# Seven-product units in the first matmul of the last two chunks of a fused attention and squared-ReLU MLP kernel, with a new order of the second matmul's products

## Chip, cores and metric

One Trainium2 chip, one core. The metric is the device time of one execution in microseconds (us). The kernel before took 306.88 us (median of three executions, 306.31 to 307.04).

## What must be computed

The reference, cut to what matters here:

```python
def reference(q, k, v, w_in, w_out):      # q, k, v: 8 batches x 8 heads x 576 x 64
    attn = _attn_ref(q, k, v)             # four heads with a sliding window, four with a dilated one
    x = attn.transpose(0, 2, 1, 3).reshape(4608, 512)
    h = x @ w_in                          # 512 -> 2048    ("mm1")
    r = np.maximum(h, 0.0)
    g = r * r
    return (g @ w_out).astype(np.float32) # 2048 -> 512    ("mm2")
```

## The kernel before

The 4608 tokens are worked in nine chunks of 512, numbered 0 to 8. Attention produces the activations batch by batch. The matmuls of a chunk are generators, and small steps of them are put between the steps of the attention of the next batch. So chunks 1 to 6 run beside attention; chunks 7 and 8 come after it and run alone.

mm1 makes `g` in 16 "p tiles": four matmuls of 512 columns into one bank of PSUM, a relu on ScalarE (ACT), a square on VectorE (DVE):

```python
def mm1_gen(c, g, sm=None):
    for ffc in range(NFF):                                   # 16 tiles
        ph = pmool.tile([P, TOKC], FP32, ..., tag="pm")      # pmool rotates four banks
        for n, dmk in enumerate((2, 3, 0, 1)):
            nc.tensor.matmul(ph, wi[:, dmk, ffc * P : ffc * P + P], xs[:, dmk, :], ...)
        relu_squared(c, ffc, g, ph, rts)
        # ... sums of g for mm2 between the tiles ...
```

mm2 is already a Strassen scheme of seven products. The first product of `a` is read out, and then a second one is added to it in the same bank; so it is with `b`. I write the order of the products as **a d b a b c e**:

```python
a = bank("poa")                                        # bank(): a tile of pmool, tag "pm"
yield from product(a, gv[:, :, 0, 0:HT], B11, True)    # first product into a
nc.scalar.copy(s1, a)                                  # readout by ACT
d_ = bank("pod");  yield from product(d_, gv[:, :, 1, HT:TOKC], T[:, 3], True)
b_ = bank("pob");  yield from product(b_, sm[:, 1], T[:, 1], True)
nc.vector.tensor_add(u2, b_, s1)                       # readout by DVE
yield from product(a, gv[:, :, 1, 0:HT], B21, False)   # second product into a
nc.scalar.copy(otu[:, :, left], a)
yield from product(b_, sm[:, 2], T[:, 2], False)       # second product into b
nc.vector.tensor_add(u3, b_, s1)
nc.vector.tensor_add(otl[:, :, left], d_, u3)
c_ = bank("poc");  yield from product(c_, sm[:, 0], T[:, 0], True)
nc.vector.tensor_add(u2, c_, u2)
nc.vector.tensor_add(otl[:, :, right], c_, u3)
e_ = bank("poe");  yield from product(e_, sm[:, 3], B22, True)
nc.vector.tensor_add(otu[:, :, right], e_, u2)
```

Two PSUM pools matter. `pmool` has four buffers of one bank, shared by mm1, mm2 and some tiles of attention (the transposes `px` and `py` among them). `papool` has two buffers of two banks each, used by attention alone.

The softmax here doesn't subtract the row's maximum and nothing guards it: scores larger than these inputs give would overflow.

## Time and profile before

| | before |
|---|---|
| time, median | 306.88 us |
| span in the trace | 305.5 us |
| TensorE (PE) busy | 296.3 us, 97% |
| a chunk beside attention (chunks 2 to 5, mean) | 30.88 us |
| chunk 7, chunk 8 | 26.04, 26.06 us |

The span is the time from the first to the last instruction on the core; the chain of waits follows what ended last backwards through it. A chunk is measured from the first mm1 matmul of its own in that chain to the first of the next chunk.

These lines are from the timeline of the kernel before, in chunk 5 (start, length, engine, line, operation, result and sources, count, and the idle time before it):

```profile
207.26 0.62 ACT L467 COPY s<-poa 128x512 f32<-128x512 f32 x1
...
209.67 1.04 PE L438 MATMUL poa<-wo,g 128*128 128x256 f16 x8
209.69 0.69 DVE L475 TENSOR_TENSOR u<-pob,s 128x512 f32<-128x512 f32 x1
...
211.93 1.04 PE L438 MATMUL pob<-T,sm 128*128 128x256 f16 x8
...
214.14 0.69 DVE L484 TENSOR_TENSOR u<-pob,s 128x512 f32<-128x512 f32 x1
...
216.45 1.04 PE L438 MATMUL poe<-wo,sm 128*128 128x256 f16 x8
```

The readout of `a` ends at 207.88, and `a`'s second product begins at 209.67: 1.8 us to spare. The readout of `b` ends at 210.38, its second product begins at 211.93: 1.55 us to spare. The readout of `b`'s second product ends at 214.83, and `e` begins at 216.45: 1.6 us, with `c` in between. A product takes 1.75 us where mm2 runs alone and about 2.25 us here, where steps of attention stand between its halves. So each slack is less than one product, and taking away the product that stands in between uses it up.

### The profile page before, as it was taken

Reading aid. Unit: us, or ns where it says so; the run is one execution under the profiler, and the core shown is the slowest. Engines: PE = TensorE matmul, PEld = TensorE weight load, DVE = VectorE, ACT = ScalarE, POOL = GpSimd, SP = SyncE. Lnnn points to the kernel's source line nnn. Section 1 sums busy time; section 2 is a strip of 40 time slices with the busy share of each in tenths; the row PEclk is TensorE's granted clock in tenths of the full one; section 3 lists DMA queues with packets and bytes.
Section 4 is the critical chain, followed back from the end, with each engine's and each line's share of the span. In section 5 each row is a group of like instructions: output and inputs, shape, how many; then the busy total and the mean of one; then the engine's idle time right before and its main releaser. Section 6 shows DMA issues by size and latency. Waiting matters only on the chain.

```text
span 305.5 us, 7013 instructions
## 1 busy us (share of the span) xinstructions
PE 296.3 (97%) x2898; PEld 192.8 (63%) x2898; DVE 208.8 (68%) x410; ACT 185.0 (61%) x308; POOL 48.5 (16%) x97
## 2 busy tenths in 40 slices
PE   8899998999999999999999999999999999999994
PEld 3675444444696469646964697459745974684584
DVE  4653475849966797679766977697769775843744
ACT  6466777478834893489348943894389437405610
POOL 7454013006004100320032003200100010000000
PEclk9999999999999999999999999999999999999999
DMA  8999989899899998689939983989310012003004
GB/s 175 226 213 230 233 174 203 160 232 269 210 191 219 310 170 185 217 182 198 228 111 197 216 184 123 213 184 209 117 72 0 2 61 78 2 0 137 2 0 138
DMA packets 85615, 47.89 MB, mean 157 GB/s; under 512 B 68112, under 2 KB 82896, under 8 KB 85200
## 3 DMA queue, kind: packets, MB, share of 16 engines
q1 hardware_dynamic: 76688, 27.24, 40.8%
q0 software_dynamic: 8352, 19.80, 28.9%
q8 instruction: 22, 0.36, 0.5%
q10 hardware_dynamic: 544, 0.43, 0.5%
q14 instruction: 9, 0.07, 0.1%
HBM read 39.85 MB, written 16.52 MB: 184 GB/s over the span
## 4 chain that ended last, share of the span: by engine, by line
PE 90%; ACT 3%; DMA 3%; POOL 2%; issue 1%; DVE 1%; ACTq 0%; POOLq 0%
PE ph L388 42%; PE pob L438 9%; PE poa L438 9%; PE poe L438 5%; PE poc L438 5%; PE pod L438 4%; PE po L409 4%; DMA early<-in_q_dram 3%; PE paw L776 3%; PE pav L759 2%; PE pz L675 2%; PE ps L656 1%; PE py L809 1%; PE px L791 1%; POOL early L119 1%; ACT AT L628 1%
## 5 line engine op out<-in xcount | busy, mean ns | idle before, releaser
L388 PE MATMUL ph<-xT,wi 128*128 128x512 f16 x576 | 129.8, 379 | 0.0
L354 ACT ACTIVATE rt<-ph 128x512 f16<-128x512 f32 x144 | 84.9, 601 | 36.4 <-PE ph L388 36.1
L388 PEld LDWEIGHTS <-wi 128*128 128x128 f16 x576 | 54.4, 98 | 62.4
L358 DVE TENSOR_TENSOR g<-rt 128x1024 f16<-128x1024 f16 x63 | 43.5, 691 | 47.2 <-ACT rt L354 47.0
L438 PEld LDWEIGHTS <-sm 128*128 128x128 f16 x512 | 46.9, 98 | 4.8
L438 PEld LDWEIGHTS <-g 128*128 128x128 f16 x384 | 35.9, 98 | 6.9 <-DVE g L356 1.3
L438 PE MATMUL pob<-T,sm 128*128 128x256 f16 x256 | 32.5, 272 | 0.0
L438 PE MATMUL poa<-wo,g 128*128 128x256 f16 x256 | 32.4, 273 | 0.0
L458 POOL DMA_DIRECT2D out_dram<-otl x6 | 4.6, 763 | 152.6 <-DVE otl L493 152.6
L815 ACT COPY xT<-py 128x576 f16<-128x576 f16 x16 | 10.2, 640 | 27.3 <-PE py L809 27.3
L740 DVE TENSOR_TENSOR x_d<-paw,rcp_d 72x512 f16<-72x512 f32 x32 | 22.0, 687 | 1.1
L797 ACT COPY xT<-px 128x576 f16<-128x576 f16 x16 | 10.3, 642 | 13.6 <-PE px L791 13.6
L409 PE MATMUL po<-wo,g 128*128 128x512 f16 x64 | 17.8, 379 | 0.0
L735 DVE RECIPROCAL rcp_d<-paw 72x8 f32<-72x8 f32 x32 | 6.4, 199 | 16.2 <-PE paw L776 16.2
L628 ACT ACTIVATE AT<-pz 128x576 f16<-128x576 f32 x28 | 16.6, 652 | 1.0 <-PE pz L675 0.6
L628 ACT ACTIVATE AT<-ps 128x576 f16<-128x576 f32 x28 | 16.6, 649 | 0.5
L740 DVE TENSOR_TENSOR x_p<-pav,rcp_p 96x512 f16<-96x512 f32 (+1 forms) x24 | 16.2, 676 | 0.8
L438 PE MATMUL poe<-wo,sm 128*128 128x256 f16 x128 | 16.3, 273 | 0.0
L438 PE MATMUL pod<-T,g 128*128 128x256 f16 x128 | 16.3, 272 | 0.0
L438 PE MATMUL poc<-T,sm 128*128 128x256 f16 x128 | 16.2, 272 | 0.0
L478 ACT COPY otu<-poa 128x512 f32<-128x512 f32 x8 | 4.7, 586 | 17.5 <-PE poa L438 17.5
L629 DVE TENSOR_TENSOR AT<-AT,maskd 128x576 f16<-128x576 f16 x28 | 12.2, 455 | 3.5 <-ACT AT L628 2.5
(120 smaller groups left out, 354.5 us busy)
## 6 DMA issues: line engine op xcount, KB each, us to landing
sv<-in_v_dram SPq DMA_DIRECT2D x40, 128.0 KB, 3.1
sd<-in_v_dram SPq DMA_DIRECT2D x8, 512.0 KB, 6.2
dk<-in_k_dram POOLq DMA_DIRECT2D x12, 288.0 KB, 7.0
dk<-in_q_dram POOLq DMA_DIRECT2D x12, 288.0 KB, 7.5
out_dram<-otl POOLq DMA_DIRECT2D x6, 512.0 KB, 3.3
out_dram<-otu POOLq DMA_DIRECT2D x6, 512.0 KB, 4.2
sd<-in_v_dram SPq DMA_DIRECT2D x8, 288.0 KB
wi<-in_moe_w_in_dram POOLq DMA_DIRECT2D x4, 512.0 KB, 10.3
```

What stands on the lines that cost most here:

```text
L354: nc.scalar.activation(rt[:, o, :], ph[:], ACTF.Relu)
L358: nc.vector.tensor_mul(g[:, ffc - 1 : ffc + 1, :], rt, rt)
L388: nc.tensor.matmul(ph, wi[:, dmk, ffc * P : ffc * P + P], xs[:, dmk, :], start=(n == 0), stop=(n == NDM - 1),)
L409: nc.tensor.matmul(po, g[:, ffc, t * P : (t + 1) * P], wo[:, ffc, :], start=(ffc == 0), stop=(ffc == NFF - 1),)
L438: nc.tensor.matmul(acc, lhs[:, k, t * P : (t + 1) * P], rhs[:, k, :], start=(first and k == 0), stop=(k == NK - 1), skip_group_check=True,)
L628: nc.scalar.activation(AT[:, u, 0:UW], ps[:, :, 0 : UW // 2], ACTF.Exp, scale=scale)
L629: nc.vector.tensor_mul(AT[:, u, 0:UW], AT[:, u, 0:UW], mask)
L735: nc.vector.reciprocal(rcp[0:w, 0:n], pv[:, :, :, D])
L740: nc.vector.tensor_tensor(out=x[0:w, 0:n], in0=pv[:, :, :, 0:D], in1=rcp[0:w, 0:n].unsqueeze(3).to_broadcast([w, n, HH, D]), op=ALU.mult,)
L776: nc.tensor.matmul(pav[:, e, h * (D + 2) : h * (D + 2) + D + 1], AT[:, u, off : off + P], vd[:, t, 2 * a + e, h, 0 : D + 1], start=True, s ...
L797: nc.scalar.copy(xT[:, 0:2, t0 : t0 + 288], px[:, 0:UW].rearrange("x (c t) -> x c t", c=2),)
L815: nc.scalar.copy(xT[:, 2:4, t0 : t0 + 288].rearrange("x c (i r) -> x c i r", r=DIL), py[:, 0:UW].rearrange("x (c r i) -> x c i r", c=2, r= ...
```

## The change

In mm1 of chunk 7, three groups of four tiles of `g`, and in chunk 8 two, are done as "units": seven products of four 256-column matmuls in place of 16 matmuls of 512 columns. Units need sums of quarters of `w_in` (four for each unit, done late in attention), sums of quarters of x, and more readouts. mm2 gets the order **a d a b c b e** in chunks 1 to 7, so that the sums of `g` are wanted later. The diff, cut to its core:

```diff
+    units = {NTOKC - 2: 3, NTOKC - 1: 2}
+    def w_in_sums(u): ...          # four DVE sums: s1..s4, 128x512 fp16 each
+    def x_sums(c): ...             # four DVE sums: t1..t4
+    def unit_gen(c, u, g):
+        both = papool.tile([P, 2, 2, HT], FP32, name=f"pu{c}_{u}", tag="pa")
+        a, d = both[:, 0], both[:, 1]
+        product(a, w(0, 0), x_quarter(c, 0, 0), True)
+        nc.scalar.copy(m1, a)
+        e = pmool.tile([P, 2, HT], FP32, name=f"pe{c}_{u}", tag="pm")
+        product(e, w(0, 1), x_quarter(c, 1, 0), True)
+        nc.vector.tensor_add(g1[:, :, first], e, m1)
+        product(a, s2, t2, False)
+        nc.scalar.copy(m6, a)
+        product(d, s1, t1, True)
+        finish(g1[:, :, first])                      # relu on ACT, square on DVE
+        product(a, s3, t3, False)
+        nc.scalar.copy(m7, a)
+        nc.vector.tensor_add(g2[:, :, second], d, m7)
+        product(a, w(1, 1), t4, False)
+        nc.scalar.activation(g2[:, :, first], a, ACTF.Relu)
+        product(d, s4, x_quarter(c, 1, 1), False)
+        nc.vector.tensor_add(g1[:, :, second], d, m6)
+        ...
+    orders = {2: "p01010p10p10p1psspspsp", 3: "01010p102120p12p2ssp2ss", ...}
...  (mm2)
-        b_ = bank("pob")                             # b's first product
-        yield from product(b_, sm[:, 1], T[:, 1], True)
-        ...
         yield from product(a, gv[:, :, 1, 0:HT], B21, False)
         nc.scalar.copy(otu[:, :, left], a)
+        if not last:
+            b_ = bank("pob"); ...                    # b's first product, now behind a's second
+            c_ = bank("poc"); ...                    # c, now ahead of b's second
         yield from product(b_, sm[:, 2], T[:, 2], False)
-        c_ = bank("poc"); ...
...  (attention of the last batch)
+        def fill():
+            pump(2)
+            if b == B - 1:
+                for _ in range(2):
+                    next(late_sums, None)            # two sums of w_in behind each step
```

In `orders` a digit is a step of that unit, `p` a p tile, `s` a sum of `g`.

More of the change, by code (lines that the diff above doesn't have):

```diff
@@ L60 @@
     tp = ctx.enter_context(tc.tile_pool(name="tp", bufs=1))
+    kp = ctx.enter_context(tc.tile_pool(name="kp", bufs=1))
     osb = ctx.enter_context(tc.tile_pool(name="osb", bufs=4))
@@ L73 @@
     wo = wpool.tile([P, NFF, DM], FP16, name="wo")
-    QKTp = [const.tile([P, 2, PADP + S], FP16, name=f"QKTp{hp}") for hp in range(2)]
+    QKTp = [kp.tile([P, 2, PADP + S], FP16, name=f"QKTp{hp}", tag=f"k{hp}") for hp in range(2)]
     QKTd = const.tile([P, 2, 2, KPAD + S], FP16, name="QKTd")
-    QKTx = const.tile([P, 2, PADP + HH * S], FP16, name="QKTx")
+    QKTx = kp.tile([P, 2, PADP + HH * S], FP16, name="QKTx", tag="kx")
     AT = const.tile([P, 8, 640], FP16, name="AT")
@@ L406, in mm1_gen, with w_in_sums, quarter @@
             yield
+    units = {NTOKC - 2: 3, NTOKC - 1: 2}
+    HU = 2 * P
+    ws0 = const.tile([P, 4, 2, HU], FP16, name="ws0")
+    ws: list = [ws0]
+    def w_in_sums(u):
+        def quarter(i, j):
+            f0 = 4 * P * u + HU * i
+            return wi[:, 2 * j : 2 * j + 2, f0 : f0 + HU]
+        s1, s2, s3, s4 = (ws[u][:, i] for i in range(4))
+        nc.vector.tensor_add(s1, quarter(1, 0), quarter(1, 1))
+        yield
+        nc.vector.tensor_sub(s2, s1, quarter(0, 0))
+        yield
+        nc.vector.tensor_sub(s3, quarter(0, 0), quarter(1, 0))
+        yield
+        nc.vector.tensor_sub(s4, quarter(0, 1), s2)
+        yield
@@ new lines, in w_in_sums_late, with x_quarter, x_sums @@
+    def w_in_sums_late():
+        wx = kp.tile([P, 2, 4, 2, HU], FP16, name="wsx", tag="kx")
+        ws.extend((wx[:, 0], wx[:, 1]))
+        for u in (0, 1, 2):
+            yield from w_in_sums(u)
+    xsums = {}
+    def x_quarter(c, j, i):
+        t0 = c * TOKC + HT * i
+        return xT[:, 2 * j : 2 * j + 2, t0 : t0 + HT]
+    def x_sums(c):
+        t = [kp.tile([P, 2, 2, HT], FP16, name=f"xs{c}_{n}", tag=f"k{n}") for n in range(2)]
+        t1, t2, t3, t4 = t[0][:, 0], t[0][:, 1], t[1][:, 0], t[1][:, 1]
+        xsums[c] = t1, t2, t3, t4
+        nc.vector.tensor_sub(t1, x_quarter(c, 0, 1), x_quarter(c, 0, 0))
+        nc.vector.tensor_sub(t2, x_quarter(c, 1, 1), t1)
+        nc.vector.tensor_sub(t3, x_quarter(c, 1, 1), x_quarter(c, 0, 1))
+        nc.vector.tensor_sub(t4, x_quarter(c, 1, 0), t2)
@@ new lines, in unit_gen, with w, product, part @@
+    def unit_gen(c, u, g):
+        t1, t2, t3, t4 = xsums[c]
+        s1, s2, s3, s4 = (ws[u][:, i] for i in range(4))
+        f0 = 4 * u
+        g1, g2 = g[:, f0 : f0 + 2, :], g[:, f0 + 2 : f0 + 4, :]
+        first, second = slice(0, HT), slice(HT, TOKC)
+        def w(i, j):
+            c0 = P * f0 + HU * i
+            return wi[:, 2 * j : 2 * j + 2, c0 : c0 + HU]
+        def product(acc, lhs, rhs, start):
+            for n in range(2):
+                for k in range(2):
+                    nc.tensor.matmul(
+                        acc[:, n, :],
+                        lhs[:, k, n * P : (n + 1) * P],
+                        rhs[:, k, :],
+                        start=(start and n == 0 and k == 0),
+                        stop=(k == 1),
+                        skip_group_check=True,
+                    )
+        def part(name):
+            return osb.tile([P, 2, HT], FP32, name=f"{name}{c}_{u}", tag="u")
+        both = papool.tile([P, 2, 2, HT], FP32, name=f"pu{c}_{u}", tag="pa")
+        a, d = both[:, 0], both[:, 1]
+        def finish(x):
+            nc.scalar.activation(x, x, ACTF.Relu)
+            nc.vector.tensor_mul(x, x, x)
+        product(a, w(0, 0), x_quarter(c, 0, 0), True)
+        m1 = part("m1")
+        nc.scalar.copy(m1, a)
+        yield
+        e = pmool.tile([P, 2, HT], FP32, name=f"pe{c}_{u}", tag="pm")
+        product(e, w(0, 1), x_quarter(c, 1, 0), True)
+        nc.vector.tensor_add(g1[:, :, first], e, m1)
+        yield "stage"
+        product(a, s2, t2, False)
+        m6 = part("m6")
+        nc.scalar.copy(m6, a)
+        yield
+        product(d, s1, t1, True)
+        finish(g1[:, :, first])
+        yield "stage"
+        product(a, s3, t3, False)
+        m7 = part("m7")
+        nc.scalar.copy(m7, a)
+        nc.vector.tensor_add(g2[:, :, second], d, m7)
+        yield "stage"
+        product(a, w(1, 1), t4, False)
+        nc.scalar.activation(g2[:, :, first], a, ACTF.Relu)
+        yield
+        product(d, s4, x_quarter(c, 1, 1), False)
+        nc.vector.tensor_mul(g2[:, :, first], g2[:, :, first], g2[:, :, first])
+        nc.vector.tensor_add(g1[:, :, second], d, m6)
+        yield "stage"
+        finish(g2[:, :, second])
+        finish(g1[:, :, second])
@@ new lines, with mm1_units_gen @@
+    orders = {
+        1: "0p0p0p0p0" + "p" + "sp" * 4 + "ppp",
+        2: "p01010p10p10p1psspspsp",
+        3: "01010p102120p12p2ssp2ss",
+    }
+    def mm1_units_gen(c, g, sm, nu):
+        if c not in xsums:
+            x_sums(c)
+        xs = xT[:, :, c * TOKC : (c + 1) * TOKC]
+        rts = {}
+        stages = [unit_gen(c, u, g) for u in range(nu)]
+        sums = hidden_sums(g, sm, 0, NK // 2)
+        ffc = 4 * nu
+        for step in orders[nu]:
+            if step == "p":
+                ph = pmool.tile([P, TOKC], FP32, name=f"ph{c}_{ffc}", tag="pm")
+                for n in range(NDM):
+                    nc.tensor.matmul(
+                        ph,
+                        wi[:, n, ffc * P : ffc * P + P],
+                        xs[:, n, :],
+                        start=(n == 0),
+                        stop=(n == NDM - 1),
+                    )
+                    if n == 1:
+                        yield
+                relu_squared(c, ffc, g, ph, rts)
+                ffc += 1
+                yield
+            elif step == "s":
+                next(sums)
+            else:
+                for what in stages[int(step)]:
+                    yield
+                    if what:
+                        break
+        assert ffc == NFF
+        for _ in sums:
+            pass
+        for _ in hidden_sums(g, sm, NK // 2, NK):
+            pass
+        yield
@@ L471, in mm2_strassen_gen @@
         yield
-        b_ = bank("pob")
-        yield from product(b_, sm[:, 1], T[:, 1], True)
-        u2 = part("u2")
-        nc.vector.tensor_add(u2, b_, s1)
-        yield
+        if last:
+            b_ = bank("pob")
+            yield from product(b_, sm[:, 1], T[:, 1], True)
+            u2 = part("u2")
+            nc.vector.tensor_add(u2, b_, s1)
+            yield
         yield from product(a, gv[:, :, 1, 0:HT], B21, False)
@@ L481, in mm2_strassen_gen @@
         yield
+        if not last:
+            b_ = bank("pob")
+            yield from product(b_, sm[:, 1], T[:, 1], True)
+            u2 = part("u2")
+            nc.vector.tensor_add(u2, b_, s1)
+            yield
+            c_ = bank("poc")
+            yield from product(c_, sm[:, 0], T[:, 0], True)
+            nc.vector.tensor_add(u2, c_, u2)
+            yield
         yield from product(b_, sm[:, 2], T[:, 2], False)
@@ L487, in mm2_strassen_gen @@
             put(1, otl, nc.sync, left)
-        yield
-        c_ = bank("poc")
-        yield from product(c_, sm[:, 0], T[:, 0], True)
-        nc.vector.tensor_add(u2, c_, u2)
+            yield
+            c_ = bank("poc")
+            yield from product(c_, sm[:, 0], T[:, 0], True)
+            nc.vector.tensor_add(u2, c_, u2)
         nc.vector.tensor_add(otl[:, :, right], c_, u3)
         put(1, otl, out_eng, right if last else slice(0, DM))
+        if c + 1 == NTOKC - 1:
+            x_sums(c + 1)
         yield
@@ L531, in moe_gen @@
         sm = gp.tile([P, 4, NK, HT], FP16, name=f"sm{c}", tag="sm")
-        yield from mm1_gen(c, g, sm)
+        if c in units:
+            yield from mm1_units_gen(c, g, sm, units[c])
+        else:
+            yield from mm1_gen(c, g, sm)
         yield from mm2_strassen_gen(c, g, sm)
@@ L1011 @@
         pump(3)
-        attn_values(b, lambda: pump(2))
+        if b == B - 1:
+            late_sums = w_in_sums_late()
+        def fill():
+            pump(2)
+            if b == B - 1:
+                for _ in range(2):
+                    next(late_sums, None)
+        attn_values(b, fill)
         pump(1000)
```

## The prediction

> **What bounds the kernel now.** I read the page first: the busy row, the slices and the chain that ended last.
>
> ```profile
> PE 296.3 (97%) x2898; PEld 192.8 (63%) x2898; DVE 208.8 (68%) x410; ACT 185.0 (61%) x308; POOL 48.5 (16%) x97
> ...
> PE   8899998999999999999999999999999999999994
> ...
> PE 90%; ACT 3%; DMA 3%; POOL 2%; issue 1%; DVE 1%; ACTq 0%; POOLq 0%
> ```
>
> TensorE (PE) is busy 97% and is 90% of the chain, so only matmul time removed, or a new wait put in front of a matmul, moves the end. Next, the chain in order of time, at its last pieces: chunk 7 (first five lines) and the end of chunk 8 (last two).
>
> ```profile
> 249.50 13.81 PE ph L388 x64
> 263.32 1.75 PE poa L438 x16
> 265.06 1.75 PE pod L438 x16
> 266.81 1.75 PE pob L438 x16
> 268.56 1.75 PE poa L438 x16
> ...
> 298.09 1.75 PE poc L438 x16
> 299.84 1.76 PE poe L438 x16
> ```
>
> The columns are start, length, group and count. So mm1 of a chunk is 64 matmuls in 13.81 us, 0.216 us each at 512 columns. A Strassen product of mm2 is 16 matmuls of 256 columns in 1.75 us, 0.109 us each. A chunk is 13.81 + 7 x 1.75 = 26.06 us, and nothing waits in it. Third, the busy time of each engine by stage: attention with chunk 6's mm2, chunk 7's mm1, chunk 7's mm2.
>
> ```profile
> 234.17:249.34 15.17, 15.17 (x198) 13.66 (x196) 12.72 (x26) 7.63 (x11) 0.00 (x0) 1.00 0.01 2
> 249.34:263.15 13.81, 13.81 (x66) 6.27 (x64) 7.98 (x13) 8.96 (x15) 1.45 (x2) 1.00 0.20 76
> 263.15:275.38 12.23, 12.23 (x114) 10.96 (x112) 6.77 (x11) 1.77 (x3) 0.00 (x0) 1.00 0.00 1
> ```
>
> After the length the columns are PE, PE's weight loads, VectorE (DVE), ScalarE (ACT). PE is full in all; DVE has only 2.4 us left in the first. Last, the durations of single operations, from the groups of the last 56 us by shape, and two pieces of the timeline:
>
> ```profile
> L354 ACT ACTIVATE rt<-ph 128x512 f16<-128x512 f32 x32 | 19.1, 597 | 14.6 <-PE ph L388 14.6
> ...
> L343 DVE TENSOR_TENSOR sm<-g 128x1024 f16<-128x1024 f16 x4 | 2.8, 692 | 0.1
> ...
> L356 DVE TENSOR_TENSOR g<-rt 128x512 f16<-128x512 f16 x4 | 1.7, 426 | 1.2 <-ACT rt L354 1.2
> ...
> L475 DVE TENSOR_TENSOR u<-pob,s 128x512 f32<-128x512 f32 x2 | 1.4, 691 | 3.2 <-PE pob L438 3.2
> ```
>
> The two pieces of the timeline (start, length, engine, operation, idle before it):
>
> ```profile
> 227.79 1.09 ACT L354 ACTIVATE rt<-ph 128x512 f16<-128x512 f32 x2
> ...
> 250.40 0.60 ACT L354 ACTIVATE rt<-ph 128x512 f16<-128x512 f32 x1 [1.10 <-PE ph L388]
> ```
>
> An ACT evacuation of 512 columns lasts 0.60 us; two queued ones take 1.09, so the next starts after 0.50. Four matmuls begun at 249.34 are issued by 250.20 and ACT starts at 250.40: 0.20 us from PE to ACT. DVE: 0.43 for 512 fp16 values, 0.69 for 1024 fp16 or for 512 from PSUM; in queued rows of the timeline the next starts 0.08 before the end. I use 0.03 to 0.05 us from ACT or DVE to the next engine.
>
> [...]
>
> **The change part by part.**
>
> *Removed.* A group is 16 matmuls of 512 (16 x 0.2158 = 3.45 us); a unit is 28 of 256 (28 x 0.1094 = 3.06). It saves 0.39; five units save **1.95 us**, all on the bounding engine.
>
> *Added on ACT and DVE.* A unit has 7 ACT ops (three copies m1, m6, m7, four relus) instead of 4, and 7 DVE ops (three adds from PSUM, four squares) instead of 2. Chunk 7 then needs in mm1 about 25 x 0.50 = 12.5 us of ACT, and on DVE 4 x 0.40 (sums of x) + 9 x 0.62 + 12 x 0.38 + 1.4 + two sums of g at 0.65 = 14.4 us, against 12.6 us of PE work. Both engines that had been 58 to 65% busy become as full as PE.
>
> *Added: a wait inside each unit.* I compared the order of instructions and the waits of both builds. Each unit's a and d are halves of one PSUM tile, and the first matmul of d = S1 T1 waits for the ACT copy m6 of a, though it writes d; likewise d += S4 x22 (the last quarter of x) waits for the ACT relu of a. Each such pair has a product of a immediately ahead, so PE must sit through 0.20 (PE to ACT) + 0.60 (ACT) + 0.05 = **0.85 us**, twice a unit. Ten times: 8.5 us. Interleaving the other unit does not help: it is not between these two products.
>
> *Moved: twelve sums of w_in* go into the last attention values, two after each step, at 0.35 to 0.46 each: 4.5 us into 2.4 of room. I walked DVE's queue with the durations above from the last sum of g (start 237.44). x_p2, on which the transposes px need, is done at 240.63 instead of 239.8: PE 0.2 late. The fourth step's sums and the fifth's stand together, so x_d of step d0_1 is done at 247.5 instead of 245.1. The paw after it needs the buffer that this frees: PE 1.4 later. Then py_1 waits for the bank that u3 frees (250.4): 0.7 more. Sum **+2.3 us**.
>
> *Chunk 7, walked the same way* (PE starts at 0; a pair of products takes 0.875, a p tile 0.863). Pairs for units 0 and 1 run to 1.75. M6 of unit 0 ends 2.19, its copy 2.99, d runs 3.04 to 3.48 (0.85 lost). Unit 1: a to 3.92, d from 4.77 (0.85). Then M7 and p to 6.51, M7 of unit 1 to 6.95. ACT runs late now: m7 of unit 0 done 6.45, the add on it 7.17, so unit 0's last a starts at 7.22 (0.27 lost), d at 8.51 (0.85). Unit 2 needs unit 0's tile, which the add d + m6 frees at 9.84: 0.94 lost. Unit 1's last d: 0.85; unit 2's first d: 0.85, PE at 14.22. Two p and M7 to 16.38; m7 of unit 2 stands behind four relus and a p on ACT, done 17.38, its add 18.1: 1.77 lost. Last d: 0.85; last p ends 20.74. In mm2 the second product waits for the last square of unit 2 (23.15): 0.27. Lost: 6 x 0.85 + 0.27 + 0.94 + 1.77 + 0.27 = 8.35; saved 3 x 0.39 = 1.17; **+7.2 us**.
>
> *Chunk 8*, two units among eight p tiles: 4 x 0.85, about 0.05 more at one of them, 0.27 before unit 0's last a, and 1.0 in the first product of mm2, which comes to tiles 12 and 14 before ACT (about 3 us behind) and DVE have squared them. Lost 4.75, saved 0.78: **+4.0 us**. The later order of mm2's products in chunks 1 to 7 moves no PE work and should cost nothing there.
>
> *Sum:* 306.9 + 2.3 + 7.2 + 4.0 = 320.4; I say **320.0 us**.
>
> **The rivals.** *First, the saving comes through.* PE is 97% busy and the units are interleaved to hide ACT; then 306.9 - 1.95 = 304.9. Against it stand the waits in the build: even with every other queue infinitely fast, ten times 0.85 less 1.95 gives 313.4. *Second, ACT and DVE throughput bind, and the waits inside the units are mostly covered by that.* Chunk 7's DVE work of 14.4 us plus about 1 us of start would end mm1 about 2 us later than now, chunk 8 about even, the attention stage +2.3: some 311. For it: both engines are nearly full. Against: PE's order is fixed, so a wait of PE also starves ACT of work; waits add, not overlap. *Third, my walk compounds too much:* if ACT's relus from SBUF are faster than evacuations, or the DVE sums cost nothing at the end of attention, I lose the 1.77, 0.94 and 2.3 but keep the ten waits: about 315.
>
> **Range and chances.** The floor from the ten waits is 313.4, already 2.1% over; all terms give 320.4. Chains longer than walked ([...]ACT working off its lag slower) add up to 4. So 315 to 324. Faster needs the waits not to exist: 0.01. Within 2% (up to 313.0) needs a mistake about half of them: 0.06. Slower: 0.93.
>
> **What would show it.** The profile after should have PE's idle time at the matmuls of d released by ACT (copies m6, relus of g), ten times, near 0.85 us each; a larger wait before unit 2's first and last a, released by DVE; ACT and DVE over 85% busy in chunk 7's mm1; matmul time down by 2 us; chunk 7 about 33 us long, chunk 8 about 30; PE gaps at paw and py in the last attention. If PE shows no gap there, the step of the shared tile is wrong; if mm1 of chunk 7 takes 16 us instead of 20.7, the queue walk is too pessimistic; if the attention stage keeps its 15.2 us, DVE's room was misjudged.

Of the range, the "up to 4" for longer chains remains as the author's estimate. The 0.03 to 0.05 us from ACT or DVE to the next engine is an estimate, too; the trace of the kernel before shows 0.03 from a relu on ACT that ends at 251.87 to the DVE operation at 251.90.

## The result

The changed kernel took **327.13 us** (median of four executions, 326.49 to 332.15), the kernel before 306.81 in the same rounds. The ratio is 1.0658 (95% interval 1.0625 to 1.069). Ratios here are the mean time of one kernel's fast runs over that of the other's of the same rounds, so not quite the ratio of the medians. One execution of the four, at 332.15 with a clock of 0.988, is left out of the ratio; the median of the three fast ones is 326.55, and differences from the changed kernel are taken from it below. The direction was predicted; the time lies 7 us above the prediction and outside its range of 315 to 324.

The page of the kernel after (busy row, PE and clock slices, shares of the chain):

```profile
PE 299.8 (92%) x2958; PEld 199.4 (61%) x2958; DVE 227.3 (70%) x455; ACT 191.8 (59%) x323; POOL 48.5 (15%) x97
...
PE   7999998999899999999999999999999765997995
PEclk9999999999999999999999999999999999799999
...
PE 59%; ACT 13%; DVE 12%; DMA 10%; issue 4%; SPq 1%; POOL 0%; ACTq 0%; POOLq 0%; DVEq 0%
```

PE falls from 97% to 92%, and from 90% of the chain to 59%: ACT and DVE now stand in the path. The slices with 7, 6, 5 are mm1 of chunk 7. The clock, at 9 throughout before, has one 7. PE's busy time rose by 3.5 us although there is less matmul work: some 1.5 us of it is that slice, and where a wait follows, four 256-column matmuls are recorded with 0.60 us in place of the 0.44 that they take in a row.

The chain of the kernel after, cut to where the chunks start (start, length, group, count): chunk 6, chunk 7, its last p tile and first mm2 product, chunk 8, the last product.

```profile
224.31 5.18 PE ph L391 x24
...
257.49 0.44 PE pu L469 x4
...
277.62 1.71 PE ph L537 x4
279.33 2.42 PE poa L593 x16
...
292.23 0.86 PE ph L537 x4
...
320.58 1.76 PE poe L593 x16
```

From such starts in both kernels comes the balance (us):

| stage | before | after | difference | predicted |
|---|---|---|---|---|
| up to chunk 1 | 63.41 | 62.64 | -0.77 | 0 |
| chunk 1 | 31.70 | 33.38 | +1.68 | 0 |
| chunks 2 to 5 | 123.52 | 128.29 | +4.77 | 0 |
| chunk 6 with the last attention | 30.87 | 33.18 | +2.31 | +2.3 |
| chunk 7 | 26.04 | 34.74 | +8.70 | +7.2 |
| chunk 8 | 26.06 | 30.11 | +4.05 | +4.0 |
| after its last product | 3.90 | 3.56 | -0.34 | 0 |
| span | 305.5 | 325.9 | +20.4 | +13.5 |

Chunks 1 to 5, whose mm1 the change does not touch, lose 6.45 us: a mean of 1.19 for each of chunks 2 to 5. That is the part that was not predicted. What PE waits for in the kernel after, over the whole run (line waited for; us in total, times, longest):

```profile
PE pu L469 <- ACT g L509: 3.5, 5, 0.7
PE pu L469 <- ACT m L498: 3.4, 5, 0.7
PE poe L593 <- DVE u L652: 2.6, 5, 0.5
PE poa L593 <- ACT s L622: 2.6, 6, 0.8
PE pu L469 <- DVE g L506: 1.9, 3, 1.6
...
PE pu L469 <- DVE g L513: 0.8, 1, 0.8
PE paw L948 <- DVE x_d L912: 0.7, 1, 0.7
...
PE poa L593 <- DVE g L359: 0.7, 1, 0.7
```

The first two lines are the ten waits inside units, the next two are new waits in mm2 beside attention. In that stretch the kernel before has none at mm2. One of the ten, in the timeline (chunk 7, unit 0; `pu` is the tile that holds `a` and `d`):

```profile
259.14 0.61 PE L469 MATMUL pu<-xs,ws 128*128 128x256 f16 x4
...
259.79 0.59 ACT L498 COPY m<-pu 128x512 f32<-128x512 f32 x1 [0.32 <-DVE xs L453]
...
260.42 0.60 PE L469 MATMUL pu<-xs,ws 128*128 128x256 f16 x4 [0.67 <-ACT m L498]
```

The product of `a` is followed by the copy of `a`, and only then by the product of `d`. The profile gives 0.67 us of idle time from the modelled end of the matmuls; from issue to issue it is 0.85, since four matmuls begun at 259.14 would let the next begin at 259.58 (4 x 0.109). And one of the new waits, in chunk 5's mm2:

```profile
211.75 0.62 ACT L622 COPY s<-poa 128x512 f32<-128x512 f32 x1
...
212.41 1.03 PE L593 MATMUL poa<-wo,g 128*128 128x256 f16 x8 [0.35 <-ACT s L622]
```

The same readout of `a` as above, with `a`'s second product now one place earlier: the slack of 1.8 us has become a wait of 0.35.

### The profile page after: what moved, and what is told of

Read it like the earlier page. It is cut to its first block, busy times and chain, and to the rows that moved or that the text cites. A ratio compares the mean times of both kernels' runs of the same rounds, so it can differ in the third digit from the quotient of the medians.

```text
span 325.9 us, 7202 instructions
## 1 busy us (share of the span) xinstructions
PE 299.8 (92%) x2958; PEld 199.4 (61%) x2958; DVE 227.3 (70%) x455; ACT 191.8 (59%) x323; POOL 48.5 (15%) x97
## 4 chain that ended last, share of the span: by engine, by line
PE 59%; ACT 13%; DVE 12%; DMA 10%; issue 4%; SPq 1%; POOL 0%; ACTq 0%; POOLq 0%; DVEq 0%
PE ph L391 24%; DMA sq<-in_k_dram 7%; PE poa L593 5%; PE pob L593 5%; PE poe L593 5%; PE pu L469 4%; DVE x_d L912 3%; PE po L564 3%; DMA wi<-in_moe_w_in_dram 3%; ACT vp L169 3%; PE poc L593 2%; ACT vd L169 2%; ACT AT L800 2%; ACT rt L357 1%; PE ps L828 1%
## 5 line engine op out<-in xcount | busy, mean ns | idle before, releaser
L391 PE MATMUL ph<-xT,wi 128*128 128x512 f16 x448 | 101.8, 380 | 0.0
L357 ACT ACTIVATE rt<-ph 128x512 f16<-128x512 f32 x124 | 72.8, 601 | 34.4 <-PE ph L391 21.5
L391 PEld LDWEIGHTS <-wi 128*128 128x128 f16 x448 | 41.9, 98 | 47.7
L361 DVE TENSOR_TENSOR g<-rt 128x1024 f16<-128x1024 f16 x53 | 36.6, 691 | 36.8 <-ACT rt L357 36.3
L593 PE MATMUL poa<-wo,g 128*128 128x256 f16 x256 | 33.4, 276 | 3.4 <-ACT s L622 2.6
```

What stands on the lines that cost most here:

```text
L357: nc.scalar.activation(rt[:, o, :], ph[:], ACTF.Relu)
L361: nc.vector.tensor_mul(g[:, ffc - 1 : ffc + 1, :], rt, rt)
L593: nc.tensor.matmul(acc, lhs[:, k, t * P : (t + 1) * P], rhs[:, k, :], start=(first and k == 0), stop=(k == NK - 1), skip_group_check=True,)
```

## The experiments

The theory after the result: **(T1)** the new order of mm2 costs about 7 us beside attention; **(T2)** the shared PSUM tile costs the ten waits; **(T3)** the sums of `w_in` cost about 2 us in the last attention; **(T4)** the rest of chunk 7 is a drop of the clock. The rival to T1 was that the additional buffers or sums disturb attention, with the order innocent.

### e1_order_only: the kernel before, with the new order alone

```diff
-        b_ = bank("pob"); ...           # a d b a b c e
+        if last: b_ = bank("pob"); ...
         yield from product(a, ..., B21, False)
+        if not last: b_ = bank("pob"); ...; c_ = bank("poc"); ...     # a d a b c b e
         yield from product(b_, sm[:, 2], T[:, 2], False)
```

> The kernel before with only the new order of mm2's products in chunks 1 to 7 (second product of a before those of b and c), no units. Theory (from the trace after: chunks 1 to 5 each take 32.07 us instead of 30.88 because the second product of a waits 0.35 us for the copy of a, which stands behind the casts of V on ScalarE, and the second product poe waits for u3, which now holds a PSUM bank longer, 0.8 us): 6 chunks x 1.19 = 7.1 us more, 313.9 us. Rival: the early chunks lost for another reason (new pool of SBUF tiles, placement), then this stays at 306.8.

Measured: 314.35 us (314.01 to 314.67) against 306.89, ratio 1.0245 (1.023 to 1.0261). Chunks 2 to 6 take 32.07 us instead of 30.88, chunk 1 takes 33.37 instead of 31.70, chunk 7 its old 26.04. What PE waits for there:

```profile
PE poe L438 <- DVE u L497: 3.2, 6, 0.5
PE poa L438 <- ACT s L467: 2.6, 6, 0.8
```

This settles T1: the order alone costs 7.5 us, with the two waits of the changed kernel, six times each, once a chunk. `a`'s second product comes one product after its first, while ACT still has attention's work ahead of the readout (in the kernel before it casts V until the copy of `a` begins at 207.26); and `e` stands directly behind `b`'s second product, whose readout frees the bank that `e` takes. In chunk 7, alone on the chip, the same order costs nothing.

### e2_old_order: the changed kernel, old order in chunks 1 to 6

```diff
+        early = c != NTOKC - 2
-        if last:
+        if early:            # b's first product ahead of a's second, c behind b's second
```

> The changed kernel with the old order of mm2's products in chunks 1 to 6 (chunk 7 and 8 as changed). Theory: gives back 5 x 1.19 in chunks 1 to 5 and up to 1.2 in chunk 6: 320 us, near what the prediction said. Rival (order innocent): 327.

Measured: 320.55 us (319.56 to 322.98), ratio 1.0459 (1.041 to 1.0508). This is the kernel that the prediction in fact computed, and it takes the predicted 320 (the walk's sum was 320.4). Chunks 2 to 5 are back at 30.88 us. The last stage of attention is 32.89, so the sums of `w_in` alone cost 2.0. Chunk 7 takes 33.30, which is 7.26 more than before; the walk in the prediction said 7.2.

It also isolates T4. The changed kernel's chunk 7 was 1.44 us longer with the same waits. The windows show it (start:end, length, then busy time of PE, its weight loads, DVE, ACT, POOL, then the granted clock, DMA share, GB/s), first for the changed kernel:

```profile
272.00:275.50 3.50, 1.96 (x12) 0.97 (x10) 3.10 (x8) 3.30 (x7) 0.00 (x0) 1.00 0.01 2
...
277.00:280.50 3.50, 3.50 (x15) 1.88 (x14) 2.68 (x5) 1.14 (x3) 0.00 (x0) 0.52 0.02 5
```

and for this experiment, right after its own poorly filled stretch of chunk 7:

```profile
270.00:273.50 3.50, 3.36 (x27) 2.64 (x27) 3.12 (x7) 1.78 (x5) 0.00 (x0) 1.00 0.02 5
```

In the changed kernel PE works 1.96 us of 3.5, and soon afterwards its clock is 0.52 for about 3.5 us: the last p tile takes 1.71 us and the first mm2 product 2.42, instead of 0.86 and 1.75, together 1.52 more. In this experiment the clock stays at 1.00 after the same stretch of waits. But its four runs at clocks of 1.000, 0.999, 0.993 and 0.987 took 319.56, 319.73, 321.38 and 322.98 us, so the drop comes in some executions and not in others. That the half-idle stretch brings it on is argued, not shown.

### e3_split: `a` and `d` as two PSUM tiles

```diff
-        both = papool.tile([P, 2, 2, HT], FP32, name=f"pu{c}_{u}", tag="pa")
-        a, d = both[:, 0], both[:, 1]
+        a = tail["p"].tile([P, 2, HT], FP32, name=f"pua{c}_{u}", tag="pua")
+        d = tail["p"].tile([P, 2, HT], FP32, name=f"pud{c}_{u}", tag="pud")
...
+    pactx.close()        # attention's PSUM pool ends; its banks become the pool of a and d
+    tail["p"] = ctx.enter_context(tc.tile_pool(name="pupool", bufs=2, space=bass.MemoryType.PSUM))
```

> The changed kernel with a and d of a unit as two PSUM tiles of one bank each instead of halves of one tile; in its build the waits of d on the reader of a are gone, nothing else moves. Theory of the prediction: ten waits of 0.85 us go, but ScalarE and VectorE then bind: walking the queues without these waits leaves chunk 7 at +3.1 and chunk 8 at +0.6 over before instead of +8.7 and +4.2, and the clock no longer drops: 327.1 - 9 = 318 us. Rival (the two engines' throughput binds and the waits are covered by it): 324 or more. Rival (the waits are all there is): 327.1 - 8.5 - 1.5 (clock) - 2 = 315.

Measured: 318.13 us (317.78 to 318.64), ratio 1.037 (1.0354 to 1.0386): 8.4 less than the changed kernel's fast runs. All ten waits are gone, the results are right. So is the 0.8 (L513) before unit 2's first product, which had to wait until both halves of unit 0's tile were read. The one large wait in the units that is left (another is 0.2):

```profile
PE pua L471 <- ACT m L507: 1.6, 1, 1.6
```

That settles T2: the waits came from the shared tile and not from the data. PE writes the bank of `d` while ACT reads the bank of `a`:

```profile
288.88 0.60 PE L471 MATMUL pud<-xs,ws 128*128 128x256 f16 x4
289.08 0.59 ACT L500 COPY m<-pua 128x512 f32<-128x512 f32 x1 [0.24 <-PE pua L471]
```

Chunk 7 takes 28.00 us and chunk 8 26.75, still 1.96 and 0.69 more than before. So the units do not pay even then: ACT, and behind it DVE, runs late, and the 1.6 us above is PE waiting for the copy m7.

### e4_pool_sums: the sums of `w_in` on GpSimd

```diff
-        nc.vector.tensor_add(s1, quarter(1, 0), quarter(1, 1))
+        nc.gpsimd.tensor_add(s1, quarter(1, 0), quarter(1, 1))      # and so s2, s3, s4
```

> The changed kernel with the twelve sums of w_in on GpSimd instead of VectorE, same place in the program. Theory (VectorE's queue in the last attention is full): the stage from chunk 6's mm2 to chunk 7's first product takes 16.4 us (order alone) instead of 17.5, total 326. If GpSimd is slow (over 1 us each) the first products with S2 may wait for them. Rival: the stage's loss is the order alone, then 327 as before.

Measured: 334.6 us (334.25 to 334.86), ratio 1.0904 (1.0886 to 1.0922). A miss by 8.6 us, in the wrong direction. The timeline:

```profile
239.97 1.48 POOL L427 TENSOR_TENSOR wsx<-wsx,wi 128x512 f16<-128x512 f16 x1
240.36 1.63 DVE L347 TENSOR_TENSOR sm<-sm,g 128x1024 f16<-128x1024 f16 x1
```

GpSimd needs 1.17 to 1.60 us for a sum that takes DVE 0.42, and beside it the DVE operation takes 1.63 us instead of its usual 0.69. It ends 0.54 us after the GpSimd sum does, and the three other 128x1024 operations between 237.24 and 243.56, of 1.64 us each, end 0.55 us after one. Behind the last sum, which ends at 244.57, the next of this size takes 0.68. It looks as if DVE had stood still until each sum ended, but that is a reading of these times. PE then waited 5.1 us at once for a square of `g`. After this wait PE was slower, too: the first half of `d`'s product, at 250.09, took 1.92 us instead of 1.04. All four executions have mean clocks of 0.983 to 0.990, so part of the loss, 8.1 us against the changed kernel's 326.55, is the clock. DVE's room, the scarce thing, got smaller by giving work away.

### e5_split_old: both repairs

The edits of e2_old_order and e3_split together.

> The changed kernel with both repairs: a and d as two PSUM tiles, and the old order of mm2 in chunks 1 to 6. Theory (terms add): before 306.9 + 1.9 (sums of w_in in the last attention, as the trace of the old-order run shows: 32.73 us from chunk 6's mm1 to chunk 7's, instead of 30.87) + 1.95 (chunk 7 of the split run 28.0 instead of 26.05) + 0.7 (chunk 8 26.75) = 311.4. Rival (repairs overlap, one wait takes the place of the other): over 313.

Measured: 311.55 us (311.25 to 311.74) against 307.17, ratio 1.0147 (1.0132 to 1.0163). The two repairs add, within 0.6 us: from the changed kernel's 326.55 the order takes 6.0 (e2), the tile 8.4 (e3), and both together 15.0. What is left, some 4.4 us, is the sums of `w_in` and the lag of ACT and DVE in the units.

### e6_sums_earlier: the sums spread over earlier stages

e5 with unit 0's sums in chunk 5's mm1 and the others in chunk 6's mm1, where the profile shows idle time on DVE:

```diff
+        elif b == B - 2:
+            first = w_in_sums(0)
+            for _ in range(11):
+                pump(1)
+                if _ % 3 == 1:
+                    next(first, None)
...
+            for _ in range(7):          # and six more below
+                pump(1)
+                next(sums_of_w, None)
...
-        attn_values(b, fill)
+        attn_values(b, lambda: pump(2))
```

> As the run before, with the twelve sums of w_in moved on VectorE: four into chunk 5's mm1, eight into chunk 6's mm1, where VectorE is busy 10.8 of 15.7 us, instead of the last attention values. Theory: the 1.9 us of the attention stage go, 309.5. Rival: VectorE is late there too and the loss moves, 311.

Measured: 311.27 us (310.91 to 311.56), ratio 1.0138 (1.0119 to 1.0156). A miss; the rival that the loss only moves was right. The wait at `paw` (1.0 us in e5) is gone, and the first product of chunk 6's mm2 waits 1.5 us for a square of `g` instead. At the place tried, DVE's idle time was not free at the right moment.

### e7_two_units and e8_one_unit: how many units pay

```diff
-    units = {NTOKC - 2: 3, NTOKC - 1: 2}
+    units = {NTOKC - 1: 2}              # e7_two_units
+    units = {NTOKC - 1: 1}              # e8_one_unit; only unit 0's sums of w_in remain
```

> Both repairs, sums earlier, and units in chunk 8 alone (two). Theory: even without the false waits the two units end late on ScalarE and VectorE, +0.7 as in the split run's chunk 8: 307.6. Rival (saving comes through once the false waits are gone): 306.9 - 0.8 = 306.1.

Measured: 308.23 us (307.97 to 308.63), ratio 1.0041 (1.0027 to 1.0056), above the 307.6 that was expected. In the trace, 0.8 us are lost to the sums in attention (31.67 us from chunk 6's start to chunk 7's, against 30.87), and two units cost chunk 8 0.70 (26.76 against 26.06), as expected.

> As the run before with one unit in chunk 8, its steps each followed by a p tile. ScalarE then has 19 operations of 0.5 us in 13.4 us of matmuls and is not late. Theory: saves the 0.39 us of a unit, 306.5. Rival: the two adds and squares at the end still hold the first product of mm2, then 306.9 or more.

Measured: 306.89 us (306.29 to 307.46), ratio 0.9995 (0.998 to 1.0011), the same time. With only unit 0's sums left, and these in chunk 5's mm1, the stage of chunk 6 is back at 30.88 us, against 32.88 in e5: that bears out T3. In the trace, mm1 of chunk 8 takes 13.85 us against 13.81, though one unit saves 0.39 us of matmul time: one product was held up by a DVE operation, and starts about 0.4 us later than the one before it would have let it.

### e9_a2_early and e10_b2_late: which half of the new order costs what

Both are the kernel before with one half of the reordering. e9 has the order **a d a b b c e**, e10 has **a d b a c b e**.

```diff
+        # e9_a2_early: a's second product ahead of b's first
         yield from product(a, ..., B21, False)
         yield from product(b_, ..., T[:, 1], True)
         yield from product(b_, ..., T[:, 2], False)
+        # e10_b2_late: c ahead of b's second product
         yield from product(c_, ..., T[:, 0], True)
         yield from product(b_, ..., T[:, 2], False)
```

> The kernel before with half of the new order: the second product of a ahead of the first of b, b's second product still ahead of c's (chunks 1 to 7). Theory: only the wait for the copy of a, behind the casts of V on ScalarE, remains: 0.37 us in each of 6 chunks with attention, +2.2, 309.1 us. Rival (the two waits are one): +7.1 or 0.

> The other half: b's second product after c's, the second of a where it was. Theory: only the wait for the PSUM bank that u3 frees remains, ahead of the second transposes and poe: 0.82 us in each of 6 chunks, +4.9, 311.8 us. Rival: without the first shift VectorE has done u3 in time and nothing is lost, 306.9.

Measured: 315.62 us (315.36 to 315.73), ratio 1.0281 (1.0265 to 1.0296), and 314.38 us (314.04 to 314.69), ratio 1.0244 (1.0223 to 1.0265), against 306.78. Both miss, by 6.5 and 2.6 us. I had split the 7.5 us between the halves; each half alone costs all of it. In e9, beside the old wait of `a`:

```profile
PE pob L438 <- DVE u L492: 4.4, 7, 0.9
```

and in e10:

```profile
PE poe L438 <- DVE u L502: 3.2, 6, 0.5
PE poc L438 <- ACT otu L478: 2.5, 6, 0.4
```

In e9, `b`'s second product stands directly behind its first and must sit through the readout between them, in chunk 7 too (seven times). In e10, `c` stands directly behind `a`'s second product and takes the bank which the copy of `a` frees, and `e` stands directly behind `b`'s second. So the cost is not in one move. In each of the orders some product follows too closely on the readout of the bank that it needs. The old order was the only one of the four without such a place.

### e11_one_unit_pp and e12_one_each: one unit in a chunk

e11 takes e8 and puts two p tiles ahead of the step that had waited for DVE. e12 also does one unit in chunk 7, with the same sums of `w_in`.

```diff
-        1: "0p0p0p0p0" + "p" + "sp" * 4 + "ppp",
+        1: "0p0p0pp0p0" + "sp" * 4 + "ppp",
...
-    units = {NTOKC - 1: 1}
+    units = {NTOKC - 2: 1, NTOKC - 1: 1}         # e12_one_each only
```

> As the one-unit run, with two p tiles instead of one between the unit's third and fourth step. In that run d += S4 x22 waited 0.43 us (weight load to weight load) for the add d + m7, and this took the 0.39 us that the unit saves. Theory: the wait goes, 0.39 us (0.13%) is kept: ratio about 0.9987, 306.5 us when before is 306.9. Rival: another wait comes in its place, ratio 1.000.

Measured: 306.76 us (306.22 to 307.72) against 306.95, ratio 1.000 (0.9982 to 1.0017): inconclusive by time. In the trace, mm1 of chunk 8 takes 13.41 us, so the 0.40 is there, but the first product of mm2 then waits 0.22 longer, and the chunk takes 25.88 against 26.06.

> The same with one unit in chunk 7 as well (the same four sums of w_in serve both): twice 0.39 us saved. Theory: ratio about 0.9975, 306.1 us when before is 306.9. Rival: in chunk 7 the sums of x come only after the last attention's adds on VectorE and hold the unit's second step, ratio 0.9987 or above.

Measured: 306.33 us (306.23 to 306.77), ratio 0.9981 (0.9968 to 0.9994). Chunk 7 takes 25.96 us, chunk 8 25.88, together 0.26 less than before. That is 0.2% less than before, with an interval that ends just below 1: with the old order, separate tiles and one unit in a chunk, the scheme seems to gain a little. Two units remove 0.78 us of matmul time; the times show 0.6 of it, the two chunks in the trace only 0.26. Since the traces of these kernels begin chunk 1 as much as 1.1 us apart, a gain of this size is not firmly shown. Two units in one chunk (e7's chunk 8) or three (e3's chunk 7) cost time.

## Why the prediction was wrong

The failed step is the last sentence before its sum: "The later order of mm2's products in chunks 1 to 7 moves no PE work and should cost nothing there." It does move no PE work, and it costs 7.5 us by itself (e1) and 6.0 to 6.7 as part of the change: with the shared tile 6.0 by time (326.55 less 320.55) and 6.7 by the stages of the two traces, without it 6.6 (e3's 318.13 less e5's 311.55). The prediction looked for waits inside the new units and did not ask the same question of the reordered products: how long before this product was the bank that it needs read out? The timeline of the kernel before had the answer: 1.8 us of slack at `a`'s second product and 1.6 at `e`, each with a product of about 2.25 us in between that the new order takes away. The slack of 1.55 at `b`'s second product is the one that e9 uses up.

The other steps, one by one:

- **The ten waits of 0.85 us** were right, in number, place and size: five for m6, five for the relu of `a`. Separate tiles took them away, and 8.4 us (e3). Of the other waits in chunk 7, the largest was walked as 1.77 and measured 1.6, the one before unit 2's first product as 0.94 and 0.8 (the measured ones count from the modelled end of the matmuls, which is some 0.17 us short of the whole).
- **Chunk 7, +7.2**: e2 shows +7.26 for the same work at full clock. In the traced run of the changed kernel it was +8.70; the term that the sum lacked is the clock drop, 1.5. It is not in every execution: the two runs of the changed kernel at a clock of 0.998 took 326.5 us, against 327.72 for the traced one at 0.993.
- **Chunk 8, +4.0**: measured +4.05.
- **The attention stage, +2.3**: measured +2.31, but this agreement is partly luck. The sums alone cost 2.0 (e2) and the order 1.19 a chunk; together they should be 3.2, and the waits overlap by 0.9. The `paw` wait was there at 0.7 (1.0 in e2) where 1.4 had been walked.
- **Saved 1.95 us**: the 0.39 for a unit is seen in e11, where mm1 with one unit is 0.40 shorter.
- **The rivals**: the saving does not come through, and engine throughput does not cover the waits, since taking them away gave 8.4 us (e3). The third, that the walk compounds too much, is refuted by e2; a relu from SBUF, which it supposed might be faster than an evacuation, took 0.63 us in the trace after (L484 at 260.39), an evacuation 0.60.
- **ACT and DVE over 85% busy in chunk 7's mm1** was wrong. They are busy 12.4 and 14.2 us of 22.0, and yet late. The prediction's own walk (12.5 and 14.4 us of work in 20.7) did not give 85% either. Both stand idle in between, waiting for a PE that waits for them.

With the order's term the prediction reads 320.4 + 7.5 - 0.9 (overlap in chunk 6) = 327.0, against 326.55; in the traced run (327.72) the clock's 1.5 stands against the 1.1 that the start and the end gained.

What stays open: why the clock drops in some runs and not in others after the same stretch of waits. In the changed kernel it fell to 0.52 after 5 us (272.0 to 277.0) with PE busy 2.69 and no gap of PE above 1.62; in e2 it stayed at 1.00 after 5 us (265.0 to 270.0) with PE busy 2.83. In e4, where PE stood still for 5.1 us at once, the mean clock was 0.983 in the traced execution and below 0.991 in all four.

## What to carry to other kernels

Before you move an instruction that accumulates into a PSUM bank, measure in the timeline the slack between the readout of that bank and the next product into it, under the load that the reading engine has there; an order that does no more work can cost more than the work that it is to serve. Put independent accumulators in separate PSUM tiles, since a reader of one half of a tile held up the writer of the other half here, by 0.85 us each time. When the bounding engine is 97% busy, a saving that loads its two helpers is worth only as much as they can take without running late: here at most one unit in a chunk, since two lost 0.70 us.
